# Both accumulators of a spectral product in one tile, one multiply and add for both, and the state products in another order

## The chip, the cores and the metric

One core of a Trainium2 chip. The time is device microseconds of one execution; lower is better. The core has five engines that the text names as the profile does: PE (TensorE: matmuls, with its weight loads as PEld), DVE (VectorE), ACT (ScalarE), POOL (GpSimd, used here to issue accumulating DMAs) and SP (SyncE, which only issues DMAs).

## The reference

Two token mixers on the same x (2048 positions, 1024 channels), blended by a gate for each position:

```
g   = sigmoid((x * gate_w).sum(-1))
a   = 2 * Re(h C^T) + x * Dskip      # h[t] = Lam_bar * h[t-1] + x[t] B_bar^T, 1024 complex states
kv  = (causal 4-tap convolution of k with shift_k, per channel) * v
y   = irfft(rfft(kv, 4096) * rfft(ssm_k, 4096))[:2048] + kv * ssm_D
b   = x * y
out = g * a + (1 - g) * b
```

## The kernel before, in words

**The H3 part (y).** The 1024 channels go in eight chunks c of 128 channels. For a chunk, kv and the filter ssm_k are folded and mirrored so that the transform of length 4096 becomes small matmuls with cosine and sine tables (CF, SF). `fwd_K` (L629) and `fwd_V` (L667) run them on PE, and ACT copies the result out of PSUM as the spectra Kh and Vh. A spectrum holds two complex parts and four blocks of 512 numbers per partition, 4096 in all. `products` (L680) multiplies them on DVE. The blocks are multiplied as polynomials: accumulator 0 (tile G) takes K's part 0 times V, accumulator 1 (tile t2, in the memory of BT[3]) takes K's part 1 times V, each for four shifts a of the blocks: `mult(a, k, room)` multiplies the blocks that are left at shift a, 4096, 3072, 2048 and 1024 numbers, and an add follows for a > 0. At the end two instructions combine the accumulators and two more fill G with the sums and differences that `inverse` (L738) takes as weights on PE (psz). ACT copies psz as cv, and SP moves it to cv_scr in DRAM.

`products` is a generator: each `yield` is a point at which the caller lets other work in. In a chunk the loop at L1136 runs `steps(prod, 3)` at L1180 (three multiplications), then `run(tv)`, the rest of `times_v` (L593): it makes ev on DVE and lets POOL issue the accumulating DMA that adds lo onto ks; ev and ks are the data of the next chunk's `fwd_V` (psv). The product n1 of accumulator 0 at shift 1 is added by another such DMA, G<-wkh. Chunk 0 is done in two halves with narrower instructions (`p0`, `p1`), and chunk 7 in a section of its own from L1306, where it adds on DVE alone.

**The S5 part (a).** `Bu` (L805) makes the state products: 16 of them, product i for time block tb and state group g by the list `order` (L788), each 32 matmuls of 128x512 on PE (psum tile "both") with the tile BT[g] and x transposed, xTs[tb], as operands. ACT splits the result into U's even and odd times, `turn_U` (L894) scales the odd ones (Q), and POOL adds Q onto the even ones by an accumulating DMA (U<-Q). `scan` (L913) takes U on DVE: rotation by the tables TC and TS (A), scan (W), rotation back (hb). `Cy` multiplies hb and U with C's tiles (psy), which `turn_C` (L1276) scales on ACT. Products 0 to 8 are made during the last chunks, 9 to 15 in the loop over the scans j at L1440, by `plan` (L1390), `turned` says which U<-Q falls into which j, and `advance` (L1411) issues scan j and the first instruction of scan j + 1, A<-TCS,U.

**Order.** `put` (L92) ties each instruction to the one before it on its engine, so the order on each engine is that of the program text, and so is that of the DMAs that SP and POOL issue. `load_t` (L120) and `move` (L123) issue on SP, `gather` (L126) on POOL. All of them show as L94 in the profile, so groups are told apart by their tiles.

**Memory that is shared.** xTs[0] and xTs[3] are one buffer (`xt_first`, L78): the last block of x can be loaded only when the last product of block 0 is done. BT[2] holds Kh of the even chunks and BT[3] the second accumulator until B's tiles are loaded there (`load_BT`, L245). After the last `inverse` the H3 pools close (L1341), and on SP follow the last tiles of C (`load_CT(4)` to `(7)`, eight transposes) and the rows for the first outputs (`loads(0)` to `(2)`: pbb, xr).

Of the kernel before, what the change touches and what calls it, by code (L numbers as in the profile page):

```python
# [20 lines left out]
def kernel(  # L21
# [112 lines left out]
        return st.enter_context(tc.tile_pool(name=name, bufs=bufs, **kw))  # L134


    kv_pool = h3pool(h3, "kvh", 3)
    g_pool = h3pool(h3, "gh", 2)
    cv_pool = h3pool(h3, "cv", 2)
    tab_pool = h3pool(h3, "tab", 1)  # L140
    WK = h3pool(h3, "wkh", 1).tile([128, 2, 3072], BF16, name="wkh")
    ld = pool("ld", 3, side="right")
    ks_pool = h3pool(h3r, "ks", 2, side="right")
    eo_pool = h3pool(h3r, "eo", 1, side="right")


    zeros = WK[:, 0, 0:512]
    put("dve", nc.vector.memset, zeros, 0.0)


# [325 lines left out]
    KH, VH, GH = {}, {}, {}  # L476

    eos, kss = {}, {}

# [131 lines left out]
    whole = {}  # L611

    def spectrum(which, c):
        if which == "K" and c % 2 == 0:

            t = BT[2].rearrange("p c d q -> p (c d q)")
        elif which == "G":
            t = whole[c] = g_pool.tile([128, 4096], BF16, name="G")
        else:
            t = kv_pool.tile([128, 4096], BF16, name=which + "h", tag="kvh")  # L620
        k = 2 if c == 0 else 1
        return [t[:, h * 4096 // k:(h + 1) * 4096 // k].rearrange("p (c b f d) -> p c b f d", c=2, b=4, d=128)
                for h in range(k)]
# [55 lines left out]

    def products(c, h=0, home=u4, by_dma=True):  # L680

        if c not in GH:
            GH[c] = spectrum("G", c)
        K, Vt, G = (x[c][h].rearrange("p c b f d -> p c b (f d)") for x in (KH, VH, GH))
        w = K.shape[3]
        T2s = kv_pool.tile([128, 4096], BF16, name="t2", tag="kvh") if c == NC - 1 else BT[3].rearrange("p c d q -> p (c d q)")
        T2 = T2s[:, h * 2048:h * 2048 + 8 * w]
        W1, W2 = (WK[:, i, h * 1536:h * 1536 + 6 * w] for i in range(2))

        def mult(a, k, room, t=None):  # L690

            full = [128, 2, 4 - a, w]
            if t is None:
                t = room.rearrange("p (c b x) -> p c b x", c=2, x=w)
            tt(t, bc(K[:, k:k + 1, a:a + 1], full), Vt[:, :, 0:4 - a], ALU.mult)
            return t

        if c == 0 and h == 0:

            for f in range(2):  # L700
                k_, v_, g_ = (x[c][h][:, :, :, f] for x in (KH, VH, GH))
                tt(g_, bc(k_[:, 0:1, 0:1], [128, 2, 4, 128]), v_, ALU.mult)
        else:
            mult(0, 0, None, G)
        yield
        n1 = mult(1, 0, W1)
        if by_dma:
            gather(G[:, :, 1:], n1)
        yield
        t2 = mult(0, 1, T2)  # L710
        yield
        n2 = mult(1, 1, W2)
        if not by_dma:
            tt(G[:, :, 1:], G[:, :, 1:], n1, ALU.add)
        if c == NC - 1:
            yield
        n3 = mult(2, 1, home([128, 4 * w], BF16, "t"))
        tt(t2[:, :, 1:], t2[:, :, 1:], n2, ALU.add)
        n2 = mult(3, 1, home([128, 2 * w], BF16, "t"))
        tt(t2[:, :, 2:], t2[:, :, 2:], n3, ALU.add)  # L720
        n1 = mult(2, 0, W2[:, 0:4 * w])
        n3 = mult(3, 0, W2[:, 4 * w:])
        tt(t2[:, :, 3:], t2[:, :, 3:], n2, ALU.add)
        tt(n1[:, :, 1:], n1[:, :, 1:], n3, ALU.add)
        yield
        tt(G[:, :, 2:], G[:, :, 2:], n1, ALU.add)
        yield
        tt(t2[:, 1], G[:, 0], t2[:, 1], ALU.subtract)
        tt(t2[:, 0], G[:, 1], t2[:, 0], ALU.add)
        if c == 0 and h == 0:  # L730
            return
        lo, hi = ((t2[:, :, :, 0:256], t2[:, :, :, 256:512]) if c > 0 else
                  [T2s[:, i * 2048:(i + 1) * 2048].rearrange("p (c b x) -> p c b x", c=2, x=256) for i in range(2)])
        to = whole[c].rearrange("p (a c b x) -> p a c b x", a=2, c=2, b=4)
        tt(to[:, 0], lo, hi, ALU.subtract)
        tt(to[:, 1], lo, hi, ALU.add)

    def inverse(c):  # L738

        del GH[c]  # L740
        G = whole.pop(c).rearrange("p (a c b f d) -> p a c b f d", a=2, c=2, b=4, d=128)
        for par in range(2):
            ps = ps2([128, 2, 4, 128], "psz")
            for j in range(2):
                tl = 2 * par + j
                for fi in range(2):
                    for cc, tab in enumerate((CI, SI)):
                        mm(ps[:, j], tab[:, fi, tl * 128:(tl + 1) * 128], G[:, par, 1 - cc, :, fi],
                           fi == 0 and cc == 0, fi == 1 and cc == 1)
            cv = cv_pool.tile([128, 2, 4, 128], BF16, name="cv")  # L750
            act(cv, ps, func=ACT.Copy)
            move(cv_scr[c, :, 2 * par:2 * par + 2], cv)
            yield
# [31 lines left out]
        tt(init[tb][:, 1], q1[:, 1], q2[:, 0], ALU.add)  # L785

    Us = {}
    order = [(0, 0), (0, 1), (1, 0), (1, 1), (2, 0), (2, 1), (0, 2), (0, 3), (1, 2), (1, 3), (2, 2), (2, 3)]  # L788
    order += [(NTB - 1, g) for g in range(NG)]
    ends = consts.tile([128, 2, NG, 2, 2], BF16, name="ends")  # L790

# [13 lines left out]
    def Bu(i):  # L805
        tb, g = order[i]
        if i == 13:
            V_ = s5p["v13"].tile([128, 2, 2, HB], BF16, name="V13")
            O_ = lam_pool.tile([128, 2, 2, HB + 2], BF16, name="O13", tag="lamd")
            Us[tb, g] = V_, O_[:, :, :, 2:]  # L810
            turns_U[i] = turn_U(g, V_, O_)
            return [Bu_plain(tb, g, V_, O_, j) for j in range(2)]
        if i in (10, 11):
            if i == 10:
                s5p["u2"] = xt_pool.tile([128, 2, 2 * (4 * HB + 4)], BF16, name="U2", tag="xT")
            U = s5p["u2"][:, i - 10]
# [319 lines left out]
    for c in range(NC - 1):  # L1136
# [40 lines left out]
            step(parts)  # L1177
        step(back)
        step(tv)
        steps(prod, 3)  # L1180
        run(tv)
        step(old)
        step(tabs)
# [113 lines left out]
            tt(CT[pi], CT[pi], whole_m, ALU.add)  # L1297

    turning = [turn_C(pi) for pi in range(NP)]
    load_BT(3, 0)  # L1300
    load_BT(3, 1)
    for pi in (1, 2):
        CT[pi] = ld.tile([128, 2, D], BF16, name="CTa", tag="ld")
        load_CT(pi)
# [1 line left out]
    with tc.tile_pool(name="fin", bufs=1, side="right") as fin:  # L1306

        count = iter(range(16))

        def room(shape, dt, name):  # L1310
            return fin.tile(shape, dt, name=name, tag=f"fin{next(count)}")

        prod, back = products(c, 0, room, False), inverse(c - 1)
        run(old)
        steps(prod, 3)
        run(turns_U[3])
        run(next(tiles))
# [62 lines left out]
    def Cy(tb, tl):  # L1380
        ps = ps2([128, 2, 512], "psy")
        for g in range(NG):
# [57 lines left out]
    for j in range(NS):  # L1440
# [109 lines left out]
```

## Time and profile before

| | before |
|---|---|
| time, median of 3 runs (lowest to highest) | 382.55 us (381.49 to 382.69) |
| span of the profiled execution | 380.0 us |
| granted TensorE clock, mean | 0.999 |
| PE busy | 371.0 us (98%), 2435 matmul records |
| DVE busy | 369.6 us (97%), 595 instructions |
| ACT busy | 309.0 us (81%), 475 instructions |
| POOL busy | 78.9 us (21%), 109 instructions |

The profile is of one execution, from its first to its last instruction; the times are of whole runs, so the 2.55 us between the span and the median lie outside the first and last instruction. In a timeline row the columns are the start and the length in us, the engine, the line, the operation, the tile written and the tiles read (buffer numbers left out), the shape and how many instructions stand in the row; brackets give the idle time before it and what ended it. "SPq" is the DMA queue that SP issues to; a DMA view gives the issues, KB each, and the time from issue to landing. Matmuls are pipelined: a row's length of 0.38 us isn't the time that PE is taken, the distance between starts is.

### The profile page before, as it was taken

The page shows a single profiled execution, that of the slowest core. Times are in us where ns is not written, and L with a number is a line of the kernel's source. Part 1 is how long each engine was busy: PE and PEld are TensorE (multiplying, and loading weights), DVE is VectorE, ACT ScalarE, POOL GpSimd, SP SyncE. Part 2 cuts the span into 40 slices and gives each one's busy share as a digit, 9 for nine tenths or more (in the row PEclk, how much of TensorE's full clock was granted, in tenths as well). Part 3 has the DMA queues.
Part 4 walks back from the last instruction along what each step waited for, and adds up shares of the span by engine and source line. Part 5 has one row for each costly group of instructions (what it writes and reads, how often), then busy time and mean ns, then how long its engine had stood idle before and what let it go on. Part 6 is the DMA issues. An engine that isn't in the chain of part 4 may idle for free.

```text
span 380.0 us, 6673 instructions
## 1 busy us (share of the span) xinstructions
PE 371.0 (98%) x2435; PEld 201.2 (53%) x2469; DVE 369.6 (97%) x595; ACT 309.0 (81%) x475; POOL 78.9 (21%) x109
## 2 busy tenths in 40 slices
PE   8999999999999999999999999999999999999995
PEld 5656357575584856654454444444444444444444
DVE  8899999999999999999999999999999999999996
ACT  5879997988989999786949999996989769937621
POOL 4011030110301103021002012122415323635000
PEclk9999999999999999999999999999999999999999
DMA  7989999998999998969999999967899999999902
GB/s 168 167 112 248 213 216 227 219 195 206 226 175 192 227 177 170 184 145 151 194 206 190 204 209 253 240 137 135 158 226 181 237 254 220 153 255 155 218 0 110
DMA packets 126259, 71.78 MB, mean 189 GB/s; under 512 B 104649, under 2 KB 107601, under 8 KB 126226
## 3 DMA queue, kind: packets, MB, share of 16 engines
q1 hardware_dynamic: 112416, 45.90, 55.9%
q0 software_dynamic: 12688, 25.17, 38.9%
q10 hardware_dynamic: 1122, 0.28, 0.4%
q8 instruction: 19, 0.31, 0.3%
q14 instruction: 14, 0.11, 0.1%
HBM read 15.48 MB, written 8.39 MB: 63 GB/s over the span
## 4 chain that ended last, share of the span: by engine, by line
PE 44%; DMA 19%; DVE 17%; issue 11%; ACT 6%; POOL 1%; SPq 0%; DVEq 0%; POOLq 0%; ACTq 0%
PE both L94 16%; PE psk L94 7%; DMA U<-Q 5%; PE taps L94 5%; PE psv L94 5%; PE psz L94 4%; DMA kT<-in_B_k_dram 3%; DVE BT L94 3%; PE even L94 3%; DVE W L94 3%; PE odd L94 2%; PE foldk L94 2%; DMA ks<-lo 2%; DMA out_dram<-m 2%; DVE hb L94 2%
## 5 line engine op out<-in xcount | busy, mean ns | idle before, releaser
L94 PEld LDWEIGHTS <-BT 128*128 128x128 bf16 x640 | 62.1, 98 | 48.3 <-issue 0.2
L94 PE MATMUL both<-xT,BT 128*128 128x512 bf16 x375 | 83.0, 379 | 0.4
L94 POOL DMA_DIRECT2D U<-Q x26 | 26.4, 1027 | 82.5 <-ACT Q L94 39.9
L94 PEld LDWEIGHTS <-hb 128*128 128x128 bf16 x256 | 24.9, 98 | 30.2 <-issue 0.5
L94 PEld LDWEIGHTS <-U 128*128 128x128 bf16 x252 | 24.6, 98 | 27.4
L94 PE MATMUL psy<-CT,hb 128*128 128x512 bf16 x157 | 36.5, 379 | 0.1
L94 ACT ACTIVATE Vh<-psv 128x1024 bf16<-128x1024 f32 x32 | 30.7, 1034 | 6.2 <-PE psv L94 6.2
L94 PE MATMUL psy<-CT,U 128*128 128x512 bf16 (+1 forms) x156 | 34.7, 368 | 0.2
L94 ACT ACTIVATE U<-both 128x512 bf16<-128x512 f32 x44 | 24.2, 594 | 10.2 <-PE both L94 9.9
L94 DVE TENSOR_TENSOR_SCAN W<-rv,init,A 128x256 bf16<-128x256 f32 x48 | 32.2, 730 | 0.0
L94 POOL DMA_DIRECT2D G<-wkh x8 | 9.7, 1218 | 101.4 <-DVE wkh L94 101.4
L94 ACT ACTIVATE Q<-U,lam 128x512 bf16<-128x512 bf16 (+1 forms) x52 | 29.9, 612 | 0.0
L94 PE MATMUL psk<-eok,SF 128*128 128x384 bf16 (+1 forms) x119 | 28.2, 354 | 0.3
L94 PEld LDWEIGHTS <-SF 128*128 128x128 bf16 x184 | 18.0, 98 | 19.4 <-issue 0.7
L94 PE MATMUL psz<-G,CI 128*128 128x512 bf16 x64 | 24.3, 379 | 0.1
L94 PE MATMUL psz<-G,SI 128*128 128x512 bf16 x64 | 24.3, 379 | 0.0
L94 PE MATMUL taps<-dg,kT 128*128 128x128 bf16 (+1 forms) x352 | 22.2, 213 | 1.0 <-DMA kT<-kT 0.7
L94 PEld LDWEIGHTS <-kT 128*128 128x128 bf16 x352 | 21.7, 102 | 2.6 <-DMA kT<-in_B_k_dram 1.2
L94 PE MATMUL psy<-CTa,hb 128*128 128x512 bf16 x94 | 22.6, 379 | 0.2
L94 DVE TENSOR_TENSOR wkh<-BT,Vh 128x3072 bf16<-128x3072 bf16 (+4 forms) x20 | 21.8, 1109 | 0.0
L94 DVE TENSOR_TENSOR wkh<-Kh,Vh 128x3072 bf16<-128x3072 bf16 (+2 forms) x16 | 21.3, 1349 | 0.0
L94 PE MATMUL psy<-CTa,U 128*128 128x512 bf16 (+1 forms) x91 | 20.7, 370 | 0.1
(230 smaller groups left out, 838.0 us busy)
## 6 DMA issues: line engine op xcount, KB each, us to landing
U<-Q POOLq DMA_DIRECT2D x26, 256.0 KB, 4.9
G<-wkh POOLq DMA_DIRECT2D x6, 768.0 KB, 8.3
cv_scr<-cv SPq DMA_DIRECT2D x16, 256.0 KB, 6.0
kn<-in_B_ssm_k_dram SPq DMA_DIRECT2D x5, 512.0 KB, 4.5
v<-in_B_v_dram SPq DMA_DIRECT2D x5, 512.0 KB, 4.5
out_dram<-m SPq DMA_DIRECT2D x8, 256.0 KB, 4.3
BT<-cv_scr SPq DMA_DIRECT2D x7, 256.0 KB, 7.3
out_dram<-BT SPq DMA_DIRECT2D x7, 256.0 KB, 2.0
```

What stands on the lines that cost most here:

```text
L94: i = f(*a, **kw)
```

## The change

- The two accumulators stand in one tile `acc`, 2 x 4096 numbers per partition; each `mult(a)` makes both at once, 8192, 6144, 4096 and 2048 numbers, and the adds go over both or over one of them. Of the products at shift 1, accumulator 0's half is still added by the DMA on POOL, accumulator 1's by DVE. The final sums are written over the tile of V's spectrum.
- A chunk issues 12 DVE instructions for it and not 17 (chunk 7: 12 and not 18; the halves of chunk 0: 11 and 12, not 16 and 17): 46 fewer in the kernel. The `yield`s stand elsewhere: the loop runs `steps(prod, 2)` ahead of `run(tv)`.
- Memory: `g_pool` is gone, `kv_pool` has two buffers and not three, the scratch WK is 7168 numbers wide and not 6144; K's spectrum stands in BT[2] or BT[3], by the chunk's parity.
- So BT[3] holds the spectrum of chunk 7 and its `load_BT(3)` comes after the products that read it. The state products of group 3 go behind those of group 2: products 6 to 11 are (0,2), (1,2), (2,2), (0,3), (1,3), (2,3). `plan` makes product 9 in j = 0, 10 in j = 1, 11 in j = 2; from j = 3 on it is unchanged.
- Since (0,3), now product 9, reads xTs[0], the load of xTs[3] moves from the section of chunk 7 into the loop, behind the plan of j = 0. On SP's queue it thereby stands behind the last cv_scr, the eight transposes of C and the rows of `loads(0)` to `(2)`. Its first reader, product 12, is in j = 3.

The core of the diff:

```diff
-    kv_pool = h3pool(h3, "kvh", 3)
-    g_pool = h3pool(h3, "gh", 2)
+    kv_pool = h3pool(h3, "kvh", 2)
+    sums = h3pool(h3, "acc", 1).tile([128, 2, 4096], BF16, name="acc")
...
-    WK = h3pool(h3, "wkh", 1).tile([128, 2, 3072], BF16, name="wkh")
+    WK = h3pool(h3, "wkh", 1).tile([128, 7168], BF16, name="wkh")
...
     def spectrum(which, c):
-        if which == "K" and c % 2 == 0:
-
-            t = BT[2].rearrange("p c d q -> p (c d q)")
-        elif which == "G":
-            t = whole[c] = g_pool.tile([128, 4096], BF16, name="G")
+        if which == "K":
+            t = BT[2 + c % 2].rearrange("p c d q -> p (c d q)")
         else:
-            t = kv_pool.tile([128, 4096], BF16, name=which + "h", tag="kvh")
+            t = whole[c] = kv_pool.tile([128, 4096], BF16, name="Vh", tag="kvh")
...
+        A = sums[:, :, h * 2048:h * 2048 + 8 * w].rearrange("p k (c b x) -> p k c b x", c=2, x=w)
+
+        def mult(a, t):
+
+            if len(t.shape) == 2:
+                t = t.rearrange("p (k y) -> p k y", k=2)
+            t = t.rearrange("p k (c b x) -> p k c b x", c=2, x=w)
+            k_ = bc(K[:, :, a:a + 1], [128, 2, 8 - 2 * a, w])
+            v_ = bc(Vt[:, :, 0:4 - a].rearrange("p c b x -> p c (b x)")[:, None], [128, 2, 2, (4 - a) * w])
+            tt(t, k_, v_, ALU.mult)
             return t
...
-            mult(0, 0, None, G)
-        yield
-        n1 = mult(1, 0, W1)
+            mult(0, sums[:, :, h * 2048:h * 2048 + 8 * w])
+        yield
+        n1 = mult(1, WK[:, h * 3072:h * 3072 + 12 * w])
         if by_dma:
-            gather(G[:, :, 1:], n1)
-        yield
-        t2 = mult(0, 1, T2)
-        yield
-        n2 = mult(1, 1, W2)
-        if not by_dma:
-            tt(G[:, :, 1:], G[:, :, 1:], n1, ALU.add)
-        if c == NC - 1:
-            yield
-        n3 = mult(2, 1, home([128, 4 * w], BF16, "t"))
-        tt(t2[:, :, 1:], t2[:, :, 1:], n2, ALU.add)
-        n2 = mult(3, 1, home([128, 2 * w], BF16, "t"))
-        tt(t2[:, :, 2:], t2[:, :, 2:], n3, ALU.add)
-        n1 = mult(2, 0, W2[:, 0:4 * w])
-        n3 = mult(3, 0, W2[:, 4 * w:])
-        tt(t2[:, :, 3:], t2[:, :, 3:], n2, ALU.add)
-        tt(n1[:, :, 1:], n1[:, :, 1:], n3, ALU.add)
-        yield
-        tt(G[:, :, 2:], G[:, :, 2:], n1, ALU.add)
-        yield
-        tt(t2[:, 1], G[:, 0], t2[:, 1], ALU.subtract)
-        tt(t2[:, 0], G[:, 1], t2[:, 0], ALU.add)
+            gather(A[:, 0, :, 1:], n1[:, 0])
+        yield
+        if by_dma:
+            tt(A[:, 1, :, 1:], A[:, 1, :, 1:], n1[:, 1], ALU.add)
+        else:
+            tt(A[:, :, :, 1:], A[:, :, :, 1:], n1, ALU.add)
+        yield
+        n2 = mult(2, WK[:, 3072:7168] if c > 0 else home([128, 8 * w], BF16, "t"))
+        n3 = mult(3, home([128, 4 * w], BF16, "t"))
+        yield
+        tt(n2[:, :, :, 1:], n2[:, :, :, 1:], n3, ALU.add)
+        tt(A[:, 1, :, 2:], A[:, 1, :, 2:], n2[:, 1], ALU.add)
+        yield
+        tt(A[:, 0, :, 2:], A[:, 0, :, 2:], n2[:, 0], ALU.add)
+        yield
+        tt(A[:, 1, 1], A[:, 0, 0], A[:, 1, 1], ALU.subtract)
+        tt(A[:, 1, 0], A[:, 0, 1], A[:, 1, 0], ALU.add)
...
-    order = [(0, 0), (0, 1), (1, 0), (1, 1), (2, 0), (2, 1), (0, 2), (0, 3), (1, 2), (1, 3), (2, 2), (2, 3)]
+    order = [(0, 0), (0, 1), (1, 0), (1, 1), (2, 0), (2, 1), (0, 2), (1, 2), (2, 2), (0, 3), (1, 3), (2, 3)]
...
-        steps(prod, 3)
+        steps(prod, 2)
         run(tv)
...
-    load_BT(3, 0)
-    load_BT(3, 1)
...
         steps(prod, 2)
+        load_BT(3, 0)
+        load_BT(3, 1)
...
         run(turning[1])
-        load_xT(3)
         b10, b11 = Bu(8)
...
-    plan = ["", "B9 B10", "B11", "B12 B13 C0", "C1", "C2", "C3 B14", "B15", "G10", "G11", "G12 G13", "G20", "G21 G22 G23",
+    plan = ["B9", "B10", "B11", "B12 B13 C0", "C1", "C2", "C3 B14", "B15", "G10", "G11", "G12 G13", "G20", "G21 G22 G23",
             "", "", ""]
-    turned = dict(zip(range(3, 12), (8, 9, 4, 10, 11, 12, 13, 14, 15)))
-    turned[0] = 7
+    turned = dict(zip((1, *range(3, 12)), (9, 7, 10, 4, 8, 11, 12, 13, 14, 15)))
...
+        if j == 0:
+            load_xT(3)
```

More of the change, by code (lines that the diff above doesn't have):

```diff
@@ L144 @@
     eo_pool = h3pool(h3r, "eo", 1, side="right")
-    zeros = WK[:, 0, 0:512]
+    zeros = WK[:, 0:512]
     put("dve", nc.vector.memset, zeros, 0.0)
@@ L474, in turn_table @@
         act(TC[:, 2 * g:2 * g + 2], y, func=ACT.Sin, bias=pih, scale=-TWO_PI)
-    KH, VH, GH = {}, {}, {}
+    KH, VH = {}, {}
     eos, kss = {}, {}
@@ L680, in products @@
     def products(c, h=0, home=u4, by_dma=True):
-        if c not in GH:
-            GH[c] = spectrum("G", c)
-        K, Vt, G = (x[c][h].rearrange("p c b f d -> p c b (f d)") for x in (KH, VH, GH))
+        K, Vt = (x[c][h].rearrange("p c b f d -> p c b (f d)") for x in (KH, VH))
         w = K.shape[3]
[L686 to L695, printed above, removed]
+        A = sums[:, :, h * 2048:h * 2048 + 8 * w].rearrange("p k (c b x) -> p k c b x", c=2, x=w)
[6 more added lines that the diff above has]
+            tt(t, k_, v_, ALU.mult)
             return t
@@ L700, in products @@
             for f in range(2):
-                k_, v_, g_ = (x[c][h][:, :, :, f] for x in (KH, VH, GH))
-                tt(g_, bc(k_[:, 0:1, 0:1], [128, 2, 4, 128]), v_, ALU.mult)
+                k_, v_ = (x[c][h][:, :, :, f] for x in (KH, VH))
+                full = [128, 2, 8, 128]
+                tt(A.rearrange("p k c b x -> p k (c b) x")[:, :, :, f * 128:(f + 1) * 128], bc(k_[:, :, 0:1], full),
+                   bc(v_.rearrange("p c b d -> p (c b) d")[:, None], full), ALU.mult)
         else:
-            mult(0, 0, None, G)
+            mult(0, sums[:, :, h * 2048:h * 2048 + 8 * w])
@@ L730, in products @@
+        tt(A[:, 1, 0], A[:, 0, 1], A[:, 1, 0], ALU.add)
         if c == 0 and h == 0:
             return
-        lo, hi = ((t2[:, :, :, 0:256], t2[:, :, :, 256:512]) if c > 0 else
-                  [T2s[:, i * 2048:(i + 1) * 2048].rearrange("p (c b x) -> p c b x", c=2, x=256) for i in range(2)])
+        t2 = sums[:, 1]
+        if c > 0:
+            lo, hi = (A[:, 1, :, :, i * 256:(i + 1) * 256] for i in range(2))
+        else:
+            lo, hi = (t2[:, i * 2048:(i + 1) * 2048].rearrange("p (c b x) -> p c b x", c=2, x=256) for i in range(2))
@@ L738, in inverse @@
     def inverse(c):
-        del GH[c]
         G = whole.pop(c).rearrange("p (a c b f d) -> p a c b f d", a=2, c=2, b=4, d=128)
@@ L812, in Bu @@
             return [Bu_plain(tb, g, V_, O_, j) for j in range(2)]
-        if i in (10, 11):
-            if i == 10:
+        if i in (11, 12):
+            if i == 11:
                 s5p["u2"] = xt_pool.tile([128, 2, 2 * (4 * HB + 4)], BF16, name="U2", tag="xT")
-            U = s5p["u2"][:, i - 10]
+            U = s5p["u2"][:, i - 11]
         else:
```

## The prediction

> **What bounds the kernel now.** I read the page's busy times first, then the timeline of PE around the places that the diff touches, then the waits of PE.
>
> ```profile
> span 380.0 us, 6673 instructions
> ...
> PE 371.0 (98%) x2435; PEld 201.2 (53%) x2469; DVE 369.6 (97%) x595; ACT 309.0 (81%) x475; POOL 78.9 (21%) x109
> ```
>
> PE is busy for 98% of the span and DVE for 97%: neither has room to take up a delay. The page models the ends of matmuls, so I look at starts:
>
> ```profile
> 212.53 0.38 PE L94 MATMUL psz<-G,CI 128*128 128x512 bf16 x1
> ...
> 215.98 34.70 PE L94 MATMUL both<-xT,BT 128*128 128x512 bf16 x156
> ```
>
> The 16 inverse matmuls of the last chunk start at 212.53, and 3.45 us later, 0.216 us apart, the state products follow. These run for 34.6 us in one piece: products 9 to 13, five of 32 matmuls, so 6.92 us each. PE never stands here, and behind it the whole rest of the kernel follows in the same written order. The waits of PE from 70 to 230 us have one row on a DMA:
>
> ```profile
> PE psv L94 <- DMA ks<-lo: 0.7, 1, 0.7
> ```
>
> So PE is the bound nearly everywhere, in an order fixed by hand; a transfer that lands after its turn on PE adds its whole lateness to the end. The change leaves all 2469 weight loads and their matmuls as they are, so I ask only where it makes PE wait. The profiled span is 380.0 us; the median of the runs is 382.55, so I add 2.5 us to a span.
>
> **The change part by part.**
>
> *Fewer, wider vector instructions.* A chunk issues 12 where it issued 17, with the same elements. What an instruction costs is read from starts:
>
> ```profile
> 139.30 2.28 DVE L94 TENSOR_TENSOR G<-Kh,Vh 128x4096 bf16<-128x4096 bf16 x1
> 141.50 1.75 DVE L94 TENSOR_TENSOR wkh<-Kh,Vh 128x3072 bf16<-128x3072 bf16 x1
> 143.17 2.28 DVE L94 TENSOR_TENSOR BT<-Kh,Vh 128x4096 bf16<-128x4096 bf16 x1
> 145.37 0.68 DVE L94 TENSOR_TENSOR ev<-ks,lo 128x1024 bf16<-128x1024 bf16 x1
> ```
>
> From start to start 4096 elements take 2.20 us and 3072 take 1.67, so 1024 elements take 0.53 and the fixed part is 0.08. 46 instructions fewer in the whole kernel would be 3.7 us of DVE over 200 us; but the finished work is fed to PE, which is full, so as a gain I count nothing. What covers it is PE's own stream; if DVE were the bound, up to 3.7 us would be gained (that end is kept with the rivals).
>
> *The gathers leave later.* In before the accumulator's gather leaves after two products (2.20 + 1.67 us); now these two are twice as wide: 2.20 + 4 x 0.53 = 4.32 and 1.67 + 3 x 0.53 = 3.26 us. It is followed on POOL's queue by the gather that finishes ks for the next chunk's forward transform. In chunk 5:
>
> ```profile
> 143.55 1.20 POOL L94 DMA_DIRECT2D G<-wkh  x1 [14.95 <-DVE wkh L94]
> 146.35 0.90 POOL L94 DMA_DIRECT2D ks<-lo  x1 [1.60 <-DVE ev L94]
> ```
> ```profile
> G<-wkh POOLq DMA_DIRECT2D x1, 768.0 KB, 8.9
> ```
> ```profile
> ks<-lo POOLq DMA_DIRECT2D x1, 256.0 KB, 8.4
> ```
> ```profile
> 154.75 0.59 PE L94 MATMUL psv<-ks,SF 128*128 128x512 bf16 x2 [0.66 <-DMA ks<-lo]
> ```
>
> The issue is 4.25 us after the chunk's first product and will be at 4.32 + 3.26 + 0.38 = 7.96: 3.7 later. The gather of ks waits for ev, which comes after two wide products (7.58) instead of three (6.07): its own issue would be about 2.1 later, once POOL has issued the first for 1.2 us. The first landed at 152.4, the second at 154.7, and PE waited for it to the tenth. If the second drains behind the first, PE waits 3.7 more; if each takes its own time, 2.1. I take 3.3, because the landings are 2.3 apart where the issues are 2.8 apart. In chunk 1 there is some cover:
>
> ```profile
> 52.95 0.91 POOL L94 DMA_DIRECT2D ks<-lo  x1 [1.61 <-DVE ev L94]
> ```
> ```profile
> ks<-lo POOLq DMA_DIRECT2D x1, 256.0 KB, 7.9
> ```
> ```profile
> 62.99 0.59 PE L94 MATMUL psv<-ks,SF 128*128 128x512 bf16 x2
> ```
>
> Landed at 60.85, used at 62.99: 2.1 us of cover, so 0 (own time) to 1.6 (behind the first) is left; I take 0.7. In the other chunks I cost this at nothing; their cover is that PE shows no wait there.
>
> *Chunk 0.*
>
> ```profile
> 22.05 1.17 DVE L94 TENSOR_TENSOR ks<-ks,v 128x2048 bf16<-128x2048 bf16 x1
> ...
> 27.69 0.42 DVE L94 TENSOR_TENSOR wkh<-wkh 128x512 bf16<-128x512 bf16 x1
> 28.26 0.69 DVE L94 TENSOR_TENSOR ev<-ks,lo 128x1024 bf16<-128x1024 bf16 x1 [0.15 <-PE psv L94]
> ```
> ```profile
> 46.03 0.39 PE L94 MATMUL mirror<-ks,refl 128*128 128x512 bf16 x1 [0.37 <-DVE ks L94]
> ```
>
> ev waits for a PE row that the change doesn't move, 28.26. Between ks<-ks,v and ev DVE now has 4.5 us of products; with the new split only two are left there (2048 and 1024 elements, 1.14 + 0.61 = 1.75 us), with the rest moved behind ev. ks<-ks,v itself comes 1.2 later, since more stands ahead of it. DVE is free at 23.2 + 1.1 + 1.8 = 26.1 and stands for 2.1 us, where it stood 0.15: 1.9 us of work is late, and at 46.03 PE already waits for DVE. So 1.9 (ends 0, if DVE catches up by then, and 1.9).
>
> The stage gives 3.3 + 0.7 + 1.9 = **5.9 us**, from 2.1 to 7.2; two more on top if the add that needs the gathered accumulator (DVE reaches it 15.7 us into a chunk by the pitches, and 7.96 + 8.9 = 16.9 is its landing) holds up the final spectrum, so up to 9.2.
>
> *BT[3] and its load* move behind the last product that reads K of chunk 7.
>
> ```profile
> 187.92 2.28 DVE L94 TENSOR_TENSOR G<-Kh,Vh 128x4096 bf16<-128x4096 bf16 x1
> ```
> ```profile
> BT<-in_A_B_re_dram SPq DMA_TRANSPOSE x4, 6.1
> ```
>
> The four products of chunk 7 are 4.32 + 3.26 + 2.20 + 1.14 = 10.9 us, with other work between them some 14.5: the tile is free at 202.4, and two transposes, one behind the other, land by about 212. Its first reader is product 9, at 215.98: 4 us of cover, so nothing.
>
> *The load of x's last block* is the step that I cost highest. It fills the buffer that product 9, (0,3), reads, so it now stands inside the loop, and SP issues in order: it goes behind everything issued after the last cv_scr.
>
> ```profile
> 205.82 6.70 SPq L94 DMA_TRANSPOSE xT<-in_A_x_dram  x2
> 215.50 2.05 SPq L94 DMA_DIRECT2D cv_scr<-cv  x2
> 217.78 1.30 SPq L94 DMA_TRANSPOSE CT<-in_A_C_re_dram  x1
> ...
> 234.86 1.82 SPq L94 DMA_TRANSPOSE CT<-in_A_C_im_dram  x1
> 236.72 0.58 SPq L94 DMA_DIRECT2D pbb<-cv_scr  x1
> ...
> 238.74 1.17 SPq L94 DMA_DIRECT2D xr<-in_A_x_dram  x1
> ```
> ```profile
> L94 SPq DMA_TRANSPOSE xT<-in_A_x_dram x8: 1994/3652/5221, 34.8 to 207.9; - x8
> ```
> ```profile
> kT<-in_B_k_dram SPq DMA_TRANSPOSE x9, 4.2
> ```
> ```profile
> CT<-in_A_C_im_dram SPq DMA_TRANSPOSE x5, 7.1
> ```
>
> The queue is never idle from 215.50 to 238.74 + 1.17 = 239.91; the pair is issued then. Its first half takes the queue for 3.65 us (median; 2.0 to 5.2), the second starts at 243.6 and lands, at 4.2 to 7.1 us for a transpose, at about 249.2 (246.2 to 252.3). Product 12 is the first of the last block and loads it as weights: PE comes to it at 215.98 + 3 x 6.92 = 236.7. PE stands for **12.5 us** (9.5 to 15.6), with product 13 and all of the rest behind it. Both times hang on the last cv, so this comes on top of the stage's 5.9.
>
> *The clock after such a stand.*
>
> ```profile
> 1.19 1.46 PE L94 MATMUL raised<-wkh 128*128 128x512 bf16 x3 [1.19 <-DVE magic L94]
> ```
> ```profile
> 1.00:2.00 1.00, 0.81 (x2) 0.28 (x3) 0.97 (x5) 0.00 (x0) 1.00 (x4) 1.00 0.03 8
> ```
>
> The first matmuls of the kernel take 0.49 us each, not 0.216, though the granted-clock column says 1.00 in that window. If the six of them up to 4.4 us stand for what follows any long idle time, PE pays some 6 x 0.27 = 1.6 us; if the column is right, nothing. I take **1.5**, by the durations. The Trainium skill ("TensorE: Matmul & The Clock Gate", section on the HAM clock gate) says that the clock's default is half and that it falls back after an idle window of about 3.4 us, until as long a busy one; by it the stand would cost an estimated 1.7 us more, with the durations and against the column.
>
> *Scan 3* loses its lead: its operand is product 9, which was finished before the loop and is now made at its start.
>
> ```profile
> 238.87 0.68 DVE L94 TENSOR_TENSOR A<-TCS,U 128x1024 bf16<-128x1024 bf16 x1
> ```
> ```profile
> 219.93 2.17 ACT L94 ACTIVATE m<-CTa,mc2i 128x1024 bf16<-128x1024 bf16 x2
> ...
> 225.29 2.19 ACT L94 ACTIVATE Q<-CT,mc2i 128x1024 bf16<-128x1024 bf16 x2
> ...
> 228.59 1.14 ACT L94 ACTIVATE CT<-CT,c2r 128x1024 bf16<-128x1024 bf16 x1
> ```
> ```profile
> U<-Q POOLq DMA_DIRECT2D x26, 256.0 KB, 4.9
> ```
>
> ACT evicts product 9 by 223.5. Up to its last Q stand scalings of C (2 x 2.17, 2.19, 2 x 1.1), three evictions and six Q, about 15 us: the gather leaves at 238.7 and lands at 243.6, where DVE wants it at 238.87. DVE waits 4.7 us. As PE stands from 236.7 to 249.2, this lies under that stand and costs nothing; without the stand it is late next.
>
> **Sum**: 380.0 + 5.9 + 12.5 + 1.5 = 399.9 us of span, + 2.5 = **402.4 us**.
>
> **The rivals.**
>
> 1. *x's last block lands in time after all* (its transposes go at the shortest rows, or SP gets past the C loads sooner). Then product 12 runs on and scan 3's wait decides: 382.55 + 5.9 + 4.7 = 393.2. For it: the shortest row of this transpose is 2.0 us. Against it: eight C transposes stand ahead and none was idle.
> 2. *The gathers keep their own time* and the queue isn't first in, first out: PE waits 2.1 in chunk 5 and none in chunk 1, and chunk 0's loss is caught up: 380.0 + 2.1 + 12.5 + 1.5 + 2.5 = 398.6.
> 3. *Not slower*: DVE's fixed parts were the real bound, and the 3.7 us that go from it pull everything forward. That needs PE not to wait for the last block. The point from which this decides: the pair must be issued by 236.7 - 9.3 = 227.4, that is, the C transposes and what follows take 10 us on the queue and not 22. Then 382.55 - 3.7 + 2.1 = 381.0 with the gathers at their low end. Against it: PE is at 98%, and an earlier product doesn't shorten its stream.
>
> **How the numbers follow.** The forecast has 0.65, rival 1 0.12, rival 2 0.15, rival 3 0.05, and 0.03 is left for something worse than 409. A measurement of this kernel can tell about 0.3% from no change, 1.1 us. Rival 3 falls on both sides of that: 0.03 faster, 0.02 the same; all else is slower, 0.95. The sum's ends are 380.0 + 2.1 + 9.5 + 0 + 2.5 = 394.1 and 380.0 + 9.2 + 15.6 + 1.6 + 2.5 = 408.9. The range reaches down past rival 1's 393.2 with a gather cost at its lower half, to 391, and up to 409.
>
> **What would show it.** In the profile after: a PE wait on an xT transfer of 9 to 16 us ahead of product 12, at about 243 us, and the xT pair on SP's queue behind the last xr. PE's wait on ks<-lo in chunk 5 at 3 to 4 us, and a small one in chunk 1. DVE's ev of chunk 0 with 2 us of idle time before it. Matmuls behind the stand at about twice 0.216 us for 3 us. A<-TCS,U of scan 3 waiting for U<-Q for about 5 us. The forecast is wrong if xT's wait is missing or under 9 us; then SP's queue was not what I read it to be.

## The result, and the profile after

The changed kernel takes 404.5 us (median of 4 runs, 402.23 to 406.13) against 382.53 us: 1.058 times the time before, 95% interval 1.054 to 1.062, so 22 us longer. The forecast was 402.4 us. The span of the profiled execution is 402.0 us, 2.5 below the median as before. This execution itself took 403.76 us: on record a time is 1.73 to 1.85 us above its span, and the rest of the 2.5 us, here and in the kernel before, is the spread of the runs. Some executions of a kernel are some per cent longer at a lower granted clock; the ratios leave them out, and e7's profile, taken in one of them, is read only for which instruction waits.

The page's first lines of the changed kernel, and its row of the granted clock (each digit a fortieth of the span):

```profile
span 402.0 us, 6660 instructions
...
PE 373.9 (93%) x2469; PEld 200.3 (50%) x2469; DVE 368.8 (92%) x549; ACT 310.7 (77%) x475; POOL 81.3 (20%) x109
...
PEclk9999999999999999999999997599999999999999
```

The work is the same: PE is busy for 373.9 us (before 371.0), DVE for 368.8 with its 46 instructions fewer (before 369.6). What came is idle time. The waits of PE, in us in total, times, longest:

```profile
PE both L94 <- DMA xT<-in_A_x_dram: 16.1, 1, 16.1
PE psv L94 <- DMA ks<-lo: 4.3, 2, 2.4
PE raised L94 <- DVE magic L94: 1.2, 1, 1.2
PE psz L94 <- DVE Vh L94: 1.2, 1, 1.2
```

One wait holds most of it. The timeline of PE shows how the 22 us come together:

```profile
217.42 0.38 PE L94 MATMUL psz<-Vh,CI 128*128 128x512 bf16 x1
...
220.87 20.88 PE L94 MATMUL both<-xT,BT 128*128 128x512 bf16 x96
257.81 15.40 PE L94 MATMUL both<-xT,BT 128*128 128x512 bf16 x64 [16.05 <-DMA xT<-in_A_x_dram]
273.04 2.32 PE L94 MATMUL psy<-CTa,hb 128*128 128x512 bf16 x10
```

The last chunk's inverse starts at 217.42 and not at 212.53: the H3 stage is 4.9 us late. Products 9 to 11 follow without a gap; product 12 then stands for 16.05 us. The 64 matmuls of products 12 and 13 take 273.04 - 257.81 = 15.2 us where they took 13.8 (2 x 6.92): another 1.4. 4.9 + 16.05 + 1.4 = 22.4 us at 273.04; 0.4 of it is regained by the end. SP's queue at that place:

```profile
223.13 1.25 SPq L94 DMA_TRANSPOSE CT<-in_A_C_re_dram  x1
...
239.83 0.58 SPq L94 DMA_DIRECT2D xr<-in_A_x_dram  x1
240.51 13.34 SPq L94 DMA_TRANSPOSE xT<-in_A_x_dram  x2
```

The pair stands where the prediction put it, behind the last xr. Its issue, 240.51, is only 0.6 us behind the 239.91 read from the kernel before, although the last inverse is 4.9 us late: SP went through what stands ahead of the pair in 17.4 us (from 223.13), where it took 22.1 (217.78 to 239.91). But the pair holds the queue for 13.3 us; before it took 6.7. Behind the H3 stage DVE has two waits that it did not have before, at the first scan and at scan 3:

```profile
221.07 0.69 DVE L94 TENSOR_TENSOR A<-TCS,U 128x1024 bf16<-128x1024 bf16 x1 [7.18 <-PE psz L94]
...
254.85 0.69 DVE L94 TENSOR_TENSOR A<-TCS,U 128x1024 bf16<-128x1024 bf16 x1 [5.86 <-DMA U<-Q]
```

The second was foreseen; the first was not.

### The profile page after: what moved, and what is told of

Read it like the earlier page. It is cut to its first block, busy times and chain, and to the rows that moved or that the text cites. A ratio compares the mean times of both kernels' runs of the same rounds, so it can differ in the third digit from the quotient of the medians.

```text
span 402.0 us, 6660 instructions
## 1 busy us (share of the span) xinstructions
PE 373.9 (93%) x2469; PEld 200.3 (50%) x2469; DVE 368.8 (92%) x549; ACT 310.7 (77%) x475; POOL 81.3 (20%) x109
## 4 chain that ended last, share of the span: by engine, by line
PE 58%; issue 15%; DVE 12%; DMA 12%; SPq 1%; ACT 1%; POOL 0%; POOLq 0%
PE psy L94 28%; PE both L94 21%; DVE acc L94 5%; DMA acc<-wkh 5%; DVE wkh L94 3%; DMA xT<-in_A_x_dram 3%; PE psz L94 3%; DMA ks<-lo 2%; PE psv L94 2%; PE psk L94 2%; DMA kT<-in_B_k_dram 1%; PE foldk L94 1%; DVE t L94 1%; SPq L94 1%; DVE Vh L94 1%
## 5 line engine op out<-in xcount | busy, mean ns | idle before, releaser
L94 PE MATMUL both<-xT,BT 128*128 128x512 bf16 x384 | 85.3, 383 | 16.1 <-DMA xT<-in_A_x_dram 16.1
L94 POOL DMA_DIRECT2D U<-Q x26 | 24.5, 955 | 93.8 <-ACT Q L94 17.6
L94 DVE TENSOR_TENSOR wkh<-BT,Vh 128x6144 bf16<-128x6144 bf16 (+2 forms) x16 | 43.0, 2689 | 0.2
L94 ACT ACTIVATE Vh<-psv 128x1024 bf16<-128x1024 f32 x32 | 30.6, 1030 | 10.2 <-PE psv L94 10.2
L94 DVE TENSOR_TENSOR acc<-BT,Vh 128x8192 bf16<-128x8192 bf16 (+2 forms) x10 | 35.6, 3568 | 1.9 <-ACT Vh L94 1.9
L94 POOL DMA_DIRECT2D acc<-wkh x8 | 9.7, 1218 | 123.0 <-DVE wkh L94 123.0
L94 ACT ACTIVATE U<-both 128x512 bf16<-128x512 f32 x44 | 24.2, 594 | 12.6 <-PE both L94 12.4
L94 DVE TENSOR_TENSOR acc<-acc,wkh 128x2048 bf16<-128x2048 bf16 (+3 forms) x23 | 32.3, 1430 | 0.3
L94 ACT ACTIVATE BT<-psk 128x1024 bf16<-128x1024 f32 x31 | 30.2, 1035 | 3.0 <-PE psk L94 3.0
L94 PE MATMUL psz<-Vh,CI 128*128 128x512 bf16 x64 | 24.3, 379 | 1.2 <-DVE Vh L94 1.2
L94 PE MATMUL psz<-Vh,SI 128*128 128x512 bf16 x64 | 24.3, 379 | 0.0
L94 PE MATMUL psv<-ks,SF 128*128 128x512 bf16 x64 | 19.0, 379 | 4.3 <-DMA ks<-lo 4.3
```

Source lines behind the costliest of these rows:

```text
L94: i = f(*a, **kw)
```

## The experiments

The theory: the time is lost in three places that add up, the late block of x (most of it), the H3 stage's later gathers, and the clock behind the stand. Rivals: the block is slow by what runs beside it and not by its place; the wider products cost by themselves. Ratios are against before in the same call, with 95% intervals.

| run | what it is | ratio to before | span, us |
|---|---|---|---|
| (changed kernel) | | 1.058 (1.054 to 1.062) | 402.0 |
| e1_xt_first | block of x issued sooner | 1.033 (1.028 to 1.039) | 390.9 |
| e2_products | products alone, a flawed edit | 1.047 (1.041 to 1.053) | 398.1 |
| e3_order | order and late load alone | 1.050 (1.045 to 1.054) | 398.4 |
| e4_warm | PE kept busy in the stand | 1.054 (1.051 to 1.056) | 400.0 |
| e5_ct_by_dve | C's gathers away, two of them beside the block | one execution | 403.4 |
| e6_ks_first | ks's gather first | 1.049 (1.046 to 1.053) | 400.2 |
| e2b_products | products alone | 1.035 (1.029 to 1.041) | 392.1 |
| e7_io_first | e1, pools moved | 1.035 (1.029 to 1.041) | not compared |
| e9_pools | e1, pools in another order | 1.034 (1.024 to 1.043) | 393.0 |
| e10_products_mended | products alone, three edits | 1.003 (0.999 to 1.006) | 382.2 |
| e11_all_mended | e1 with the three edits | 1.024 (1.016 to 1.032) | 389.6 |
| e12_old_pools | e10 without one edit | 1.019 (1.014 to 1.023) | 387.9 |

**e1_xt_first: the place on SP's queue.**

```diff
-    load_CT(6)
-    load_CT(7)
     loads(1)
-    loads(2)
...
         if j == 0:
             load_xT(3)
+            load_CT(6)
+            load_CT(7)
+            loads(2)
```

> The changed kernel with one thing moved: the pair of transposes that loads x's last block is issued behind C's tiles 4 and 5 and the rows of the first two outputs, ahead of C's tiles 6 and 7 and the third output's rows. If PE's 16.1 us wait is a matter of the place on SP's queue (theory), the pair leaves SP at about 231.5 instead of 240.5, and even if it takes 13.3 us again lands by 245, 3 us after PE's turn at 241.7: PE's wait is 0 to 4 us and the time falls to 387 to 394. If it is below 1 us, scan 3's wait for U<-Q becomes visible (5 us, 392). If the place doesn't matter and the transposes are held up by what runs beside them (rival), the wait stays above 10 us and the time above 398.

SP's queue and PE's waits of this run from 230 to 262 us:

```profile
230.71 8.06 SPq L94 DMA_TRANSPOSE xT<-in_A_x_dram  x2
```
```profile
PE psy L94 <- ACT U L94: 2.8, 1, 2.8
PE both L94 <- ACT U L94: 1.2, 1, 1.2
PE both L94 <- DMA xT<-in_A_x_dram: 0.5, 1, 0.5
```

Ten us sooner on the queue, and the wait is 0.5 us in place of 16.1. The span falls by 11 us and not by 17: PE now waits 4.0 us for ACT, which evicts the products' U too late (it scales C and Q in between), and behind the longer of these two waits the granted clock falls to half, so that 12 matmuls take 4.27 us (259.38 to 263.65) where they take 2.59 elsewhere: another 1.7. DVE's wait at scan 3 is 2.1 us. So the place decides, and behind it lies the next limit.

**e3_order: the other half alone**, the kernel before with only the new order, plan and load:

```diff
-    order = [(0, 0), ..., (0, 2), (0, 3), (1, 2), (1, 3), (2, 2), (2, 3)]
+    order = [(0, 0), ..., (0, 2), (1, 2), (2, 2), (0, 3), (1, 3), (2, 3)]
...
-        load_xT(3)
...
+        if j == 0:
+            load_xT(3)
```

> The old products, and only the new order of the state products with the later load of x's last block. If the two parts add up (theory), PE waits 12 to 17 us for the block ahead of product 12 and pays 1.4 us of slow matmuls: 396 to 401. If the late block's wait has to do with the products (rival), it is under 8 us and the time under 392.

```profile
217.02 20.88 PE L94 MATMUL both<-xT,BT 128*128 128x512 bf16 x94
254.04 2.29 PE L94 MATMUL both<-xT,BT 128*128 128x512 bf16 x5 [16.14 <-DMA xT<-in_A_x_dram]
```

The same wait to 0.1 us, with the old products: the span is 398.4, 18.4 of the 22 us. The wait doesn't need the new products.

**e4_warm: the clock.**

```diff
+        if j == 3:
+            warm = ps2([128, 2, 512], "warm")
+            for _ in range(70):
+                mm(warm[:, 0], BT[0][:, 0, 0, 0:128], xTs[2][:, 0], True, True)
         for unit in plan[j].split():
```

> The changed kernel with 70 idle 128x512 matmuls (their result isn't used) on PE ahead of product 12, where it waits: 15.1 us of work in a wait of 16.1. If the eight slow matmuls behind the wait come from the clock having fallen in it (theory), they go, and the span falls by 1.4 us, from 402.0 to 400.6, with a granted clock of 1.00 throughout. If they come from the weights or the operand (rival), they stay and the span is the same or a little longer.

First the granted clock (the column behind POOL's) in the changed kernel, in windows of 2 us around the stand, which lasts from 241.8 to 257.8:

```profile
244.00:246.00 2.00, 0.00 (x0) 0.00 (x0) 1.97 (x5) 2.00 (x2) 0.78 (x2) 1.00 1.37 108
246.00:248.00 2.00, 0.00 (x0) 0.00 (x0) 1.97 (x4) 0.03 (x1) 0.14 (x1) 0.77 1.34 90
248.00:250.00 2.00, 0.00 (x0) 0.00 (x0) 0.99 (x3) 0.00 (x0) 0.00 (x0) 0.50 1.22 141
...
258.00:260.00 2.00, 2.00 (x6) 0.69 (x5) 1.94 (x5) 2.00 (x3) 0.48 (x1) 0.50 0.75 134
260.00:262.00 2.00, 2.00 (x9) 0.78 (x8) 2.00 (x5) 2.00 (x3) 0.37 (x1) 0.82 0.60 105
262.00:264.00 2.00, 2.00 (x11) 0.90 (x10) 1.97 (x4) 2.00 (x4) 0.00 (x0) 1.00 0.16 26
```

It falls to half some 5 us into the stand and comes back 3 us after PE works again. PE's timeline with the idle matmuls:

```profile
242.07 15.27 PE L94 MATMUL warm<-xT,BT 128*128 128x512 bf16 x68
257.25 13.97 PE L94 MATMUL both<-xT,BT 128*128 128x512 bf16 x63
271.06 2.75 PE L94 MATMUL psy<-CTa,hb 128*128 128x512 bf16 x12
```

The clock stays at 1.00 and the 64 matmuls take 271.06 - 257.25 = 13.8 us, not 15.2: the 1.4 us are the clock's. The span is 400.0; in the times of the runs (1.054 and 1.058) the difference doesn't stand out of the intervals, so the 1.4 us rest on these rows.

**e5_ct_by_dve: what makes the block slow.** Two of POOL's gathers for C are issued within 1.2 us of the pair in the changed kernel.

```diff
-                gather(CT[pi][:, c], m[c])
+                tt(CT[pi][:, c], CT[pi][:, c], m[c], ALU.add)
```

> The changed kernel, with C's tiles 4 and 5 finished by adds on DVE in place of four accumulating DMAs on POOL's queue. In the profile of the changed kernel two of these are issued right when the pair of x's last block is, and the second transpose of the pair then holds SP's queue for 9.5 us. If the accumulating DMAs are what slows it (theory), the pair lands in 7 to 10.5 us instead of 17.2 from its issue and PE's wait falls from 16.1 to 7 to 11 us. If the pair is slow by itself or behind C's transposes (rival), the wait stays at 15 to 17 us.

```profile
247.69 7.85 SPq L94 DMA_TRANSPOSE xT<-in_A_x_dram  x2
```
```profile
PE both L94 <- DMA xT<-in_A_x_dram: 10.5, 1, 10.5
PE psv L94 <- DMA ks<-lo: 5.4, 2, 3.2
```

Without C's gathers the pair takes 7.85 us of the queue, not 13.3, and PE has the block 10.0 us after the pair's issue (257.73 - 247.69) instead of 17.3. PE's wait falls by 5.6 us and not by 7.3, since the pair was issued 0.4 us behind PE's turn, in the changed kernel 1.3 ahead of it. Beside C's gathers the pair held the queue for 13.3, 13.9, 10.9 and 12.6 us (changed kernel, e3, e4, e6), so e5's single 7.85 lies outside their spread. What the place and the neighbours cost can't be added: in e1 the other place alone takes the wait to 0.5 us, and there C's gathers are issued only behind the pair. The span doesn't fall, since in this one execution the H3 stage ran 5.5 us later (the inverse starts at 222.91): its waits for ks were 1.1 us longer, and the granted clock fell to half behind both of them (last section). Only the pair and its wait are read from it.

**e6_ks_first: the H3 stage.**

```diff
-        steps(prod, 2)
+        step(prod)
         run(tv)
+        step(prod)
```

> The changed kernel with ev and the accumulating DMA of ks issued behind the first multiplication of a chunk and ahead of the second, so that ks is ahead of the accumulator on POOL's queue and no later than before. If the lateness of the H3 stage is that DMA's (theory), PE's waits on ks<-lo fall from 4.3 us to below 1 and the last chunk's inverse starts 3 to 4 us sooner, at 213.5 to 214.5 instead of 217.42; the wait for x's last block stays, so the time falls to 400 to 402. If the accumulator's own DMA, now later, takes its place (rival), DVE waits for it and psz for DVE, and the start stays above 216.

PE's waits from 100 to 170 us:

```profile
PE mirror L94 <- ACT TCS L94: 1.2, 1, 1.2
PE psz L94 <- DVE Vh L94: 0.8, 1, 0.8
PE mirror L94 <- DVE ks L94: 0.7, 2, 0.4
```

The waits for ks<-lo are gone, as the theory had it, but the inverse starts at 216.30 and not at 214: small waits for DVE and ACT take their place, and DVE waits 1.3 us for the accumulator's DMA, as the rival had it. Even the 1.1 us gained can't be told from chance: e1, with the H3 stage of the changed kernel, starts its inverse at 216.32. The time, 401.19 us, is as the theory had it, but 1.2 us of the gain is a shorter wait for x's block (14.8) in this execution. Neither forecast holds as a whole.

**e2_products and e2b_products: the products in the old order.** The edit: old `order`, `plan`, `turned` and loads; kv_pool with three buffers, one for the last K, and WK with 6144 numbers; and for room

```diff
-        n2 = mult(2, WK[:, 3072:7168] if c > 0 else home([128, 8 * w], BF16, "t"))
+            rooms = [WK[:, 0:4 * w] if c == NC - 1 else home([128, 4 * w], BF16, "t"), WK[:, 3072:3072 + 4 * w]]
+            n2 = [r.rearrange("p (c b x) -> p c b x", c=2, x=w) for r in rooms]
+            for k in (1, 0):
+                tt(n2[k], bc(K[:, k:k + 1, 2:3], [128, 2, 2, w]), Vt[:, :, 0:2], ALU.mult)
```

> The new products in the old order of the state products, with the old places of the loads of B's group 3 and of x's last block; K's spectrum of the last chunk gets a buffer of its own, and to make room for it the shift-2 product and its add are made in two instructions for the two accumulators. If the lateness of the H3 stage is carried to the end (theory), the inverse of the last chunk starts 4 to 5 us later than before's 212.53, and the time is 386.5 to 388. If the lateness is made up again by fewer instructions on DVE (rival), it is within 1 us of before's 382.5.

This first form used a third scratch tile in chunk 0 as well, for which DVE waited 8.1 us: a flaw of the edit, and its 398.1 says nothing on the change. With chunk 0 left as in the changed kernel (the diff above):

> The new products alone again (old order, old places of the loads), now without the third scratch tile in chunk 0 that made DVE wait for 8.1 us in the run before; chunks 1 to 7 still make the shift-2 product in two instructions for room. If the lateness of the H3 stage is carried to the end and DVE's wait for the last inverse adds to it (theory: both engines are full), the inverse of the last chunk starts at 217 to 219 and the span is 388 to 393. If that wait is free because PE's lateness covers it (rival), the span is 380 plus the lateness of the inverse alone, 385 to 387.

DVE's waits from 30 to 230 us:

```profile
DVE A L94 <- PE psz L94: 8.4, 1, 8.4
DVE acc L94 <- ACT Vh L94: 2.2, 1, 2.2
```

The inverse starts at 219.69, 7.2 us late and 0.7 outside the forecast, and the span is 392.1, 12.1 longer: behind the inverse 5 us more are lost. That speaks for the theory, that DVE's wait at the first scan isn't free once nothing longer covers it; e12 below tests this by itself.

**e7_io_first and e9_pools: that wait's place in memory.** When the H3 pools close, the scan's work pool takes over the lowest memory. Before, V's and K's spectra lay there, which DVE had finished reading; now the last spectrum, written over V, lies there, and psz reads it to the end. Both runs start from e1.

```diff
+    s5p["io"] = pool("io", 2)
     wk = pool("wk", 5)
...
-    s5p["io"] = pool("io", 2)
```

> The kernel with x's last block issued sooner, and the pool for the output rows opened ahead of the scan's work pool when the H3 memory is handed on, so that the scan's first tile no longer lies where the last spectrum is. If DVE's 7.2 us wait for psz at the first scan is a matter of that place (theory), it goes. If DVE bounds what follows, the span falls from 390.9 by 2 to 6 us; if ACT's late evictions do (rival), the wait goes and the span stays within 1.5 us of 390.9.

The wait at A goes, and another turns up at the next pool's tile, the scan's result hb:

```profile
226.33 0.69 DVE L94 TENSOR_TENSOR hb<-TCS,W 128x1024 bf16<-128x1024 bf16 x1 [7.24 <-ACT U L94]
```

The row puts its end to ACT and not to psz; what held that memory isn't shown. The time is e1's within the intervals. For e9 the pools are laid down in another order:

```diff
-    kv_pool = h3pool(h3, "kvh", 2)
     sums = h3pool(h3, "acc", 1).tile([128, 2, 4096], BF16, name="acc")
+    WK = h3pool(h3, "wkh", 1).tile([128, 7168], BF16, name="wkh")
+    kv_pool = h3pool(h3, "kvh", 2)
     cv_pool = h3pool(h3, "cv", 2)
     tab_pool = h3pool(h3, "tab", 1)
-    WK = h3pool(h3, "wkh", 1).tile([128, 7168], BF16, name="wkh")
```

> The kernel with x's last block issued sooner, and the accumulators' and the scratch pool laid down ahead of V's, so that the scan's work tiles and its results, 24 KB, fall onto memory that only DVE read (30 KB) and no longer onto the tile that psz reads last. If the memory's place makes DVE wait at the first scan (theory), the 7.2 us wait goes without turning up at another tile, and the scans run up to 7 us sooner. The span then falls from 390.9 to 385 to 389; if ACT's late evictions bound it (rival), the wait goes and the span stays at 389.5 to 392.

DVE's waits from 205 to 262 us:

```profile
DVE A L94 <- DMA U<-Q: 9.0, 1, 9.0
```

The wait is gone, and scan 3's wait has grown from e1's 2.1 to 9.0 us: DVE came there 4.8 us sooner (243.15 for 247.90), though the inverse of this execution is 3.3 us later (219.64 for 216.32), and waited there instead. The time is that of e1 within the intervals; the span, 393.0, is a little above what either forecast allows. In the new order something else is late anyway, as the rival said.

**e10, e11, e12: the parts put together.** e10 is e2b with e6's edit, e9's pool order (V's with three buffers, WK of 6144) and, for chunk 0, two more adds ahead of ev:

```diff
-            step(p0)
+            steps(p0, 2)
             run(tv)
...
             steps(p1, 2)
-            step(p0)
```

> The new products alone (old order and loads) with three edits: ks's DMA ahead of the accumulator's on POOL's queue, two more adds of chunk 0 ahead of ev, where DVE stood for 2.5 us, and the pools laid down in the other order. If these three are what the products cost (theory), the last chunk's inverse starts within 2 us of 212.53, DVE's wait at the first scan is gone and the time is 382 to 385. If the wider instructions cost by themselves (rival), the time stays above 387.

PE's waits from 20 to 215 us:

```profile
PE psz L94 <- DVE Vh L94: 1.7, 2, 1.0
PE mirror L94 <- DVE ks L94: 1.7, 5, 0.4
```

384.21 us, 1.003 times before (0.999 to 1.006): no difference that these runs can tell. The inverse starts at 215.03, half a us outside what was expected, and nothing is lost behind it. e12 is e10 with the pools as the change has them:

> The mended products without the third edit: the pools lie again as the change has them, so the scan's first tile falls on the tile that psz reads last. If that place costs time where nothing else covers it (theory), DVE waits some 5 to 7 us at the first scan again, PE waits for hb, C or U later on, and the span is 385 to 389. If the wait is free because DVE has that much room behind it (rival), the span is 381.5 to 383.5, as that of the mended products, 382.2.

```profile
DVE A L94 <- PE psz L94: 5.3, 1, 5.3
```
```profile
PE psy L94 <- ACT U L94: 1.9, 1, 1.9
PE psy L94 <- DVE CT L94: 1.3, 1, 1.3
PE psy L94 <- DVE hb L94: 1.1, 2, 0.9
```

DVE's 5.3 us at the first scan come back on PE in four waits, 4.3 us together, the first of them at 259: the span is 5.7 longer, 0.5 of it from a later inverse (215.54). The place in memory has a price of its own, shown here by one edit. e12 also parts the other two edits of e10 from the pools: it differs from e2b by them alone, its inverse starts 4.2 us sooner (215.54 for 219.69) and its span is 4.2 us shorter. So the order of POOL's DMAs and the adds of chunk 0 together cost e2b these 4.2 us; how much each does isn't shown. e11 is the changed kernel with e1's loads and the three edits:

> The changed kernel with the same three edits and x's last block issued sooner. If the four causes add up (theory), PE's wait for the block is below 2 us, those for ks below 1, and the time is 384 to 389: what is left is ACT's load after the order of the products. If the new order is dear in itself (rival), it stays above 391.

```profile
PE psy L94 <- ACT U L94: 3.2, 1, 3.2
PE both L94 <- DMA xT<-in_A_x_dram: 1.8, 1, 1.8
```
```profile
258.99 4.44 PE L94 MATMUL psy<-CTa,hb 128*128 128x512 bf16 x12 [3.21 <-ACT U L94]
263.26 4.48 PE L94 MATMUL psy<-CT,hb 128*128 128x512 bf16 x20
```

Its time, 391.92 us, is just above 391, so the rival holds: the four causes don't make up the whole, and the new order with its loads is dear in itself. Against e10's span 7.4 us stay with it, and PE's rows account for them: 1.8 us of waiting for the block, 3.9 for ACT's evictions (0.7 of it in a row not shown), and 1.7 for the clock, which is at 0.50 behind the 3.2 us wait: the 12 matmuls take 263.26 - 258.99 = 4.27 us, in e10 2.59. No version that was run beats the kernel before.

## Why the prediction was right

- **What bounds the kernel.** Right: PE's stream goes on in a fixed order, and what PE had lost by 273 us reached the end nearly whole (22.4 us there, 22.0 at the end). The fewer instructions gained nothing, as costed: e10 has 30 of the 46 fewer (565 on DVE for 595) and is as fast as before. Where DVE doesn't wait, the period of a chunk is hardly shorter: 22.9 us from one ks<-ks,v to the next (45.8 and 68.7), before 23.0 (44.75 and 67.76).
- **The block of x.** The mechanism and its size against everything else were right: PE waits for this block behind the last xr, and most of the loss is that wait. Its size, 16.05 us for 12.5 and just outside 9.5 to 15.6, is two larger errors that partly cancel, so that it came near is luck. The landing was taken from medians of transposes elsewhere: 9.3 us from the pair's issue (249.2 - 239.91), where it was 17.3, 8.0 more. The issue was to shift with the last cv like PE's turn; PE's turn did (241.76 for 236.7), the issue hardly, since the queue ahead took 17.4 us for 22.1: it came 4.3 us sooner against the late stage. 12.5 + 8.0 - 4.3 is within 0.2 us of what was measured. In the kernel before two of C's gathers (230.02 and 231.06) run beside the transposes ahead, in the changed kernel (240.58 and 241.62) beside the pair. e5 speaks for them as the reason of the long landing (10.0 us without them); whether they also slowed the queue before wasn't tested.
- **The H3 stage.** 4.9 us for 5.9, but the parts were not right, and the sum is near by luck. PE's row mirror<-ks, once a chunk, shows where the lateness arises:

| mirror<-ks starts, us | chunk 0 | 1 | 2 | 3 | 4 | 5 |
|---|---|---|---|---|---|---|
| before | 46.03 | 69.92 | 93.36 | 116.70 | 139.44 | 162.99 |
| changed | 47.08 | 70.09 | 94.24 | 119.38 | 142.38 | 167.87 |
| later by | 1.05 | 0.17 | 0.88 | 2.68 | 2.94 | 4.88 |

  Chunk 0, costed at 1.9 to the end, is all but caught up a chunk later. Most of the rest comes with the changed kernel's two waits for ks, in chunks 3 and 5:

```profile
112.45 0.59 PE L94 MATMUL psv<-ks,SF 128*128 128x512 bf16 x2 [1.97 <-DMA ks<-lo]
```
```profile
159.63 0.59 PE L94 MATMUL psv<-ks,SF 128*128 128x512 bf16 x2 [2.38 <-DMA ks<-lo]
```

  Chunk 5 is 1.7 us worse than before and not 3.3, below the 2.1 of "each takes its own time". Chunk 1, costed at 0.7, doesn't wait. Chunk 3, costed at nothing because PE showed no wait there, waits 2.0. That step failed: no wait in the trace doesn't say how much cover there is. It was 3.4 us (issue at 100.17, landing 6.2 us later, use at 109.77); the issue came 2.6 us later, and the landing took 9.6 us. In e1, whose H3 stage is the same, that landing took 7.6 us and PE waited 0.2, so this part differs from one execution to the next. The two us for the add that needs the gathered accumulator (15.7 against 16.9 is 1.2) didn't come: DVE has no wait for acc<-wkh in the changed kernel. In chunk 0 DVE stands for ev as forecast:

```profile
28.07 0.69 DVE L94 TENSOR_TENSOR ev<-ks,lo 128x1024 bf16<-128x1024 bf16 x1 [2.55 <-ACT eok L94]
```

  Rival 2, in which the gathers keep their own time and chunk 0 catches up, had 2.1 us for the stage. Its mechanism fits chunks 0, 1 and 5 better than the forecast does; the forecast is nearer with 4.9 only through chunk 3, which neither had.
- **The clock.** 1.4 us for 1.5, shown by e4. The Trainium skill ("TensorE: Matmul & The Clock Gate", section on the HAM clock gate) agrees with the column in this place: half speed after an idle window, back after some 3.4 us of work; here it came back after 2.9. The Trainium skill gives the idle window as about 3.4 us, and there the runs differ: in e5 half speed followed a wait of 2.24 us (last section), and the measurement decides.
- **Scan 3's wait** is 5.9 us for 4.7 and lies under the stand, as forecast; its size is chance too, since U<-Q took 11.6 us to land and not 4.9 and DVE came there 5 us later than reckoned, behind its wait at the first scan. When the stand was taken away, ACT's late evictions (4.0 us) were next as well; the prediction named only scan 3.
- **BT[3]'s load** costs nothing, as said: PE has no wait for it in the changed kernel (in e9 it had one of 1.0 us).
- **Not foreseen** was DVE's 7.2 us at the first scan. The prediction went through queues and products and not through which tile the next pool is laid on. Under a 16 us stand it cost nothing; alone, in the old order, it costs some 5 us of e12's 5.7.

## What to carry to other kernels

When a load is moved to wait for a buffer, its place on the issuing queue has to be worked out along with everything ahead of it, and the landing from what else is in flight at that time. A change of buffers also changes whose memory the next stage inherits: look at who reads that memory last. Where two engines are full, an idle stretch in either can come out at the end, as in e12, and a longer wait elsewhere hides it only until that one is mended. A sum that comes out near can hold errors that cancel: compare it term by term.

## What the hardware showed beyond that

- A transpose pair of the same size held its queue for 6.7, 7.85, 8.1 and 13.3 us (before, e5, e1, changed). In the changed kernel four gathers issued beside the pair (C's two, U<-Q, pbb<-gd) landed after 10.6 to 11.6 us, in e5 the U<-Q that was left beside it took 5.7. The gathers aren't the whole of it: at its old place the pair took 6.7 us in the kernel before and 9.3 to 10.2 in e2b, e10 and e12, with U<-Q and CTa<-m issued beside it in each.
- The granted clock fell with short waits too, and the length of the wait alone doesn't decide it. In e5 PE waited 3.2 us for ks, and these windows show half speed, for some 6 us:

```profile
160.00:162.00 2.00, 0.00 (x0) 0.00 (x0) 1.71 (x2) 0.00 (x0) 0.00 (x0) 0.83 1.06 128
162.00:164.00 2.00, 1.77 (x5) 0.67 (x5) 1.97 (x3) 0.73 (x1) 0.00 (x0) 0.50 1.10 211
164.00:166.00 2.00, 2.00 (x6) 0.64 (x5) 1.97 (x3) 1.32 (x2) 0.00 (x0) 0.50 1.01 191
166.00:168.00 2.00, 2.00 (x6) 0.76 (x5) 2.00 (x2) 1.03 (x2) 0.00 (x0) 0.50 1.64 211
```

  In e5 it also fell for 3.5 us right behind a wait of 2.24 us (0.50 from 113.5 to 117). In the changed kernel, with waits of 2.0 and 2.4 us, it didn't fall there, nor in e9 with one of 2.85. Behind its two waits e5's PE works at half speed for some 9 us in all; half of that, an estimated 4.6 us, goes into its later inverse. At the kernel's start the column says 1.00 while the matmuls take 0.49 us; which of them is right there stays open.
